# A fused attention and MoE kernel: one PSUM tile of two banks made two, and another order from the list scheduler

## The chip, the cores and the metric

The kernel runs on one core of a Trainium2 chip. The metric is the device time of one execution in microseconds (us); the lower the better. The engines are named as in the profile: PE is TensorE's matmuls, PEld its weight loads, DVE is VectorE, ACT ScalarE, POOL GpSimd, SP SyncE, which issues DMAs.

## What is computed

Two parts, one behind the other. Retention attention over 4 × 768 tokens, 8 heads of 64; then RMS norm and a gated layer (512 to 1536 to 512). Both in fp32.

```python
# attention, for each block b of the sequence (pos is the place in the block)
Dmask = np.where(rel >= 0, lam[:, None, None] ** rel[None, :, :], 0.0)
intra = np.einsum('bhic,bhjc->bhij', qb, kb) * Dmask[None]
intra = np.einsum('bhij,bhjd->bhid', intra, vb)
inter = np.einsum('bhid,bhde->bhie', qb * lam_pow[None], kv_state)
out[:, :, sl] = intra + inter
kv_state = lam_block[None, :, None, None] * kv_state + np.einsum('bhsd,bhse->bhde', kb_dec, vb)
...
# gated layer, x is the attention's output as 3072 x 512
rms = np.sqrt(np.mean(x * x, axis=-1, keepdims=True) + 1e-06)
xn = x / rms * rms_g
g = xn @ w_gate
silu = g * (1.0 / (1.0 + np.exp(-g)))
val = xn @ w_val
return (silu * val @ w_out).astype(np.float32)
```

## The kernel before

**Tiles and stages.** The 3072 tokens are six groups `m` of 512 (four chunks of 128, `GC`). The inner width of 1536 is twelve blocks `f` of 128. A *unit* is one `(m, f)`: it takes the group's normed tokens through block `f` of the gate and the value weights, joins both and multiplies with the block of the output weights into four accumulators `acc` (banks `po0` to `po3`). The heads go in four *pairs* `p` a group. Matrix products in fp32 precision are made from fp16 halves (a high and a low part, `x`'s, `wg`, `wv`, `wo`), so each takes three.

The first 24 units are *classical*: 12 matmuls of 512 columns into `pg` (gate) and 12 into `pv` (value). All later ones are *Strassen* units: a product with fewer matmuls from sums of the weights (`ws`, from which come the low-precision sums in `wo`, `third`, `partial`) and of the tokens. Such a unit has seven products of six matmuls with 256 columns; they go into two halves, `pa` and `pb`. The first product goes into `pa`, the second into `pb`; ScalarE copies `pa` away (`keep`, L984), VectorE adds `pb` to the copy (`sum_val`, L988), and further products follow in both.

**PSUM.** Odd Strassen units take `pa` and `pb` from the two one-bank tiles `pg` and `pv`. Even ones take both from *one* tile of two banks, tag `ps` (`pp` in the profile, L937). A pair's scores (L510) use the same two-bank tile, one bank for each head, and VectorE multiplies them with the decay mask in one instruction of 1024 columns (`decay_a`, L526). The row sums of the norm (`pss`), its spread to all partitions (`pr`), the norms of the weights (`pn`), of the output weights' columns (`pc`) and `pm` use the first bank of a `ps` tile.

**Weights.** Each block is loaded, rounded (`convert`, L231 and L234), squared and normed on TensorE (`norm_bank`: `pn`, L451), scaled; the output block's columns are squared by ScalarE (L305), added by VectorE (L311), the second time by GpSimd (L314), and summed by TensorE into `pc`, from which VectorE takes exponents (`en`, L336). Halves and low parts are made by ScalarE, VectorE (`rest_h`, L277) and GpSimd (L282); the sums `ws` by VectorE (L884 to L888).

**What sets the order.** The first six units and the eight pairs of groups 0 and 1 are a sequence written out by hand (`ramp`). Behind it a list scheduler (`Plan`) is given every step with its engine, a cost in us, a position, and what it reads, writes and opens; `run` picks steps in the order of their planned starts and issues them. Each engine then executes its queue in that order. The scheduler thinks of a bank as free 0.2 us after the last step that used it, and prices a VectorE step of its list `SHARED` higher while it plans a GpSimd step.

Of the kernel before, what the change touches and what calls it, by code (L numbers as in the profile page):

```python
# [23 lines left out]
def retention_swiglu_kernel(  # L24
# [261 lines left out]
    class Column:  # L286
# [26 lines left out]
        def last(self):  # L313
            nc.gpsimd.tensor_add(self.sq[:, :, 0], self.sq[:, :, 0], self.sq[:, :, 1])  # L314

    class Norms:
# [13 lines left out]
        def part(self, fn, i):  # L330
            self.pc = ps_att.tile([P, 2, G], F32, tag="ps", name="pc")[:, 0]
            fn(i, self.between)
# [40 lines left out]
    def spread_least():  # L373
        pm = ps_att.tile([P, 2, G], F32, tag="ps", name="pm")[:, 0, :P]
        nc.tensor.matmul(pm, least.broadcast_to([P, P]), ident, start=True, stop=True)
        return pm
# [19 lines left out]
    class Weights:  # L396
# [97 lines left out]
    class Pair:  # L494
# [9 lines left out]
        def scores(self, chunks=range(GC)):  # L504
            m, p = self.m, self.p
            if 0 in chunks:
                self.pa = ps_att.tile([P, 2, GC, P], F32, tag="ps", name=f"pa_{m}_{p}")
            for c in chunks:
                for j, r in enumerate(heads):
                    nc.tensor.matmul(  # L510
                        self.pa[:, j, c, :], self.kT[r, c, :], self.qT[r, c, :],
                        start=True, stop=True,
                    )
# [8 lines left out]
        def decay_a(self):  # L522
            p = self.p
            self.a = att.tile([P, 2, GC, P], F32, tag="a", name=f"a_{self.m}_{p}", bufs=2)
            decay = mask[:, 2 * p : 2 * p + 2, :].rearrange("p j (o i) -> p j o i", o=1)
            nc.vector.tensor_mul(self.a, self.pa, decay.broadcast_to([P, 2, GC, P]))  # L526
# [88 lines left out]
    def row_sums(m, i):  # L615

        if i == 0:
            if m:
                ps = ps_att.tile([P, 2, G], F32, tag="ps", name=f"pss_{m}")[:, 0]
# [12 lines left out]
    class Norm:  # L632
# [20 lines left out]
        def spread(self):  # L653
            if self.m:
                pr = ps_att.tile([P, 2, GC, P], F32, tag="ps", name=f"pr_{self.m}")[:, 0]
# [17 lines left out]
        def row_sums(self):  # L673

            ps = ps_att.tile([P, 2, G], F32, tag="ps", name=f"pss_{self.m}")[:, 0]
# [266 lines left out]
    class Hidden:  # L942
# [31 lines left out]
        def first(self, u):  # L974
            self.banks(u)
            self.add(1)

# [67 lines left out]
    def ramp():  # L1045
# [122 lines left out]
        w1.pn = ps_att.tile([P, 2, G], F32, tag="ps", name="pn_1")[:, 0]  # L1168
# [34 lines left out]
        w2.pn = ps_att.tile([P, 2, G], F32, tag="ps", name="pn_2")[:, 0]  # L1203
# [35 lines left out]
        w3.pn = ps_att.tile([P, 2, G], F32, tag="ps", name="pn_3")[:, 0]  # L1239
# [40 lines left out]
        w4.pn = ps_att.tile([P, 2, G], F32, tag="ps", name="pn_4")[:, 0]  # L1280
# [46 lines left out]
        w5.pn = ps_att.tile([P, 2, G], F32, tag="ps", name="pn_5")[:, 0]  # L1327
# [78 lines left out]
    class Plan:  # L1406


        LAG = {("PE", "PE"): 0.0, ("PE", "ACT"): 0.28, ("PE", "DVE"): 0.28}
        SHARED = (  # L1410
            "low", "mul_sums", "sums", "refine", "rest_high", "convert", "convert_o", "add_squares",
        )
        ENGINES = ("PE", "ACT", "DVE", "POOL", "LD", "LO", "ST")

# [33 lines left out]

        def run(self, horizon=1.3, reach=600):
            deps = self.links()  # L1450
            n = len(self.steps)
            end = [None] * n
            clock = dict.fromkeys(self.ENGINES, 0.0)
            left = list(range(n))
            live = {}
            left_of = {k: len(v) for k, v in self.users.items()}
            free_at = {t: [0.0] * b for t, b in self.tags.items()}
            tag_of = {}
            for name, tag in self.open.items():
                tag_of[name] = tag  # L1460
                free_at[tag].pop()
                if name not in left_of and name not in self.fixed:
                    free_at[tag].append(0.0)
            last = dict.fromkeys(clock, 0.0)
            progress, order = 0.0, []
            pool_until = 0.0

            def ready(i):
                eng = self.steps[i][0]
                t = 0.0  # L1470
                for d in deps[i]:
                    if end[d] is None:
                        return None
                    t = max(t, end[d] + self.LAG.get((self.steps[d][0], eng), 0.15))
                need = {}
                for name, tag in self.steps[i][7]:
                    k = need[tag] = need.get(tag, 0) + 1
                    if len(free_at[tag]) < k:
                        return None
                    t = max(t, sorted(free_at[tag])[k - 1] + 0.2)  # L1480
                return t

            while left:
                found = {}
                window = left[:reach]
                for limit in (horizon, 99.0):
                    for i in window:
                        eng, _, at = self.steps[i][:3]
                        if at > progress + limit:
                            continue  # L1490
                        if eng in ("LD", "LO") and found.get(eng):
                            continue
                        t = ready(i)
                        if t is None:
                            if eng in ("LD", "LO"):
                                found[eng] = [(at, 1e9, i)]
                            continue
                        found.setdefault(eng, []).append((at, t, i))
# [501 lines left out]
```

## Time and profile before

| | before |
|---|---|
| median of 3 runs | 671.53 us (670.36 to 672.75) |
| the profiled execution | 672.92 us, span 671.1 us |
| granted TensorE clock, mean | 0.997 |
| busy: PE, PEld | 652.8, 444.1 us |
| busy: DVE, ACT, POOL | 440.4, 330.5, 163.6 us |
| DMA | 51.12 MB, mean 76 GB/s |

Busy times are those of the profiled execution. PEld runs beside PE. A matmul's record is longer than the step to the next one, since matmuls are pipelined: 0.38 us for 512 fp16 columns at a step of some 0.21. So idle time before a matmul is what lies between the end of one record and the start of the next, and a loss is read from start to start. In a timeline a row is: start, length, engine, line, operation, output and inputs, shape, count, and in brackets the idle time of the engine before it with what ended it.

### The profile page before, as it was taken

The numbers are of one execution on the slowest core, as the hardware profiler recorded it, in microseconds if no ns is written. First come the engines' busy times: TensorE is split into PE (matmuls) and PEld (weight loads), VectorE is DVE, ScalarE is ACT, GpSimd is POOL, SyncE is SP. The second block draws the span as 40 slices with busy tenths as digits, with TensorE's granted clock in tenths as the row PEclk, the third lists the DMA queues.
The fourth block names the chain that finished last, engine by engine and source line by source line (L and its number), as shares of the span: only waits on it lengthen the run. The fifth ranks groups of instructions, "written<-read, shape, count | busy, mean of one in ns | idle before, by whom it ended". The sixth has DMA issues, their size and how long they took to land.

```text
span 671.1 us, 12372 instructions
## 1 busy us (share of the span) xinstructions
PE 652.8 (97%) x5035; PEld 444.1 (66%) x5035; DVE 440.4 (66%) x790; ACT 330.5 (49%) x672; POOL 163.6 (24%) x144
## 2 busy tenths in 40 slices
PE   8999999999999999999999999999999999999997
PEld 8846655555565555777767777767777776767774
DVE  6798869889977976767664444477644377543333
ACT  3686658676654542454453443335444434433332
POOL 2300130114776833478220011002111001100000
PEclk9999999999999999999999999999999999999999
DMA  8966626321002200211100321100230000100001
GB/s 312 346 237 213 230 79 209 113 84 64 0 3 97 91 1 33 95 63 63 65 1 1 110 79 64 64 1 1 80 111 1 1 1 1 39 26 1 1 1 63
DMA packets 14312, 51.12 MB, mean 76 GB/s; under 512 B 1712, under 2 KB 1968, under 8 KB 12848
## 3 DMA queue, kind: packets, MB, share of 16 engines
q1 hardware_dynamic: 13968, 49.69, 20.8%
q8 instruction: 39, 0.64, 0.4%
q10 hardware_dynamic: 288, 0.66, 0.4%
q14 instruction: 17, 0.14, 0.1%
HBM read 44.05 MB, written 6.29 MB: 75 GB/s over the span
## 4 chain that ended last, share of the span: by engine, by line
PE 85%; DVE 10%; ACT 2%; issue 1%; DMA 1%; POOL 0%; DVEq 0%; ACTq 0%; POOLq 0%
PE pp L937 17%; PE pa L937 9%; PE acc L779 9%; PE acc L781 8%; PE acc L780 8%; PE pv L760 7%; PE pg L760 7%; PE pb L937 7%; PE pa L510 4%; PE po L571 3%; PE po L582 3%; PE pst L539 2%; DVE tx L988 1%; PE pss L627 1%; ACT tx L984 1%
## 5 line engine op out<-in xcount | busy, mean ns | idle before, releaser
L781 PE MATMUL acc<-wo,hh 128*128 128x512 f16 (+1 forms) x288 | 111.0, 386 | 0.0
L780 PE MATMUL acc<-wo,hh 128*128 128x512 f16 (+1 forms) x288 | 111.0, 385 | 0.0
L779 PE MATMUL acc<-wo,hh 128*128 128x512 f16 x216 | 82.4, 381 | 0.2 <-DVE hh L1033 0.2
L937 PEld LDWEIGHTS <-wo 128*128 128x128 f16 x576 | 55.7, 98 | 31.4 <-issue 9.8
L760 PE MATMUL pg<-x,wg 128*128 128x512 f16 x288 | 67.6, 380 | 1.3 <-ACT sg L1008 1.1
L937 PEld LDWEIGHTS <-wg 128*128 128x128 f16 x576 | 56.3, 98 | 16.8 <-issue 0.8
L760 PE MATMUL pv<-x,wv 128*128 128x512 f16 x288 | 67.3, 379 | 0.0
L1026 ACT CAST hh<-sg 128x512 f16<-128x512 f32 (+1 forms) x72 | 44.4, 617 | 44.8 <-DVE sg L1002 20.9
L984 ACT COPY tx<-pp 128x256 f32<-128x256 f32 x72 | 26.8, 372 | 77.2 <-PE pp L937 76.2
L937 PEld LDWEIGHTS <-wv 128*128 128x128 f16 x576 | 56.2, 98 | 8.7 <-DVE xn L733 0.6
L988 DVE TENSOR_TENSOR tx<-pp,tx 128x256 f32<-128x256 f32 x48 | 20.4, 425 | 58.9 <-ACT sg L996 45.7
L530 POOL TENSOR_TENSOR qkv<-qkv,pw 128x512 f32<-128x512 f32 x22 | 30.3, 1381 | 101.6 <-PE pa L510 101.6
L984 ACT COPY tx<-pa 128x256 f32<-128x256 f32 x72 | 26.7, 371 | 53.6 <-PE pa L937 52.9
L760 PEld LDWEIGHTS <-wg 128*128 128x128 f16 x288 | 26.4, 98 | 35.2 <-issue 5.3
L760 PEld LDWEIGHTS <-wv 128*128 128x128 f16 x288 | 27.5, 98 | 33.2 <-issue 1.4
L1033 DVE TENSOR_TENSOR hh<-sg,hh 128x512 f16<-128x512 f32 x54 | 41.0, 759 | 6.3 <-ACT hh L1026 5.5
L992 DVE TENSOR_TENSOR sg<-pp,tx 128x256 f32<-128x256 f32 x24 | 10.2, 424 | 51.3 <-ACT tx L984 51.3
L937 PE MATMUL pp<-tx,wo 128*128 128x256 f16 x288 | 39.0, 272 | 5.0 <-DVE tx L988 4.4
L1002 DVE SCALAR_TENSOR_TENSOR sg<-tx,cv,sg 128x512 f32<-128x512 f32 x48 | 38.9, 811 | 3.3
L988 DVE TENSOR_TENSOR tx<-pb,tx 128x256 f32<-128x256 f32 x48 | 20.4, 424 | 28.2 <-PE pb L937 25.3
L781 PEld LDWEIGHTS <-hh 128*128 128x128 f16 x216 | 21.1, 98 | 25.5
L754 POOL TENSOR_TENSOR tx<-xt,tx 128x768 f16<-128x768 f32 x8 | 14.8, 1853 | 92.8 <-ACT tx L750 92.8
(192 smaller groups left out, 1310.1 us busy)
## 6 DMA issues: line engine op xcount, KB each, us to landing
qkv<-in_qkv_dram SPq DMA_DIRECT2D x47, 512.0 KB, 4.7
raw_gv<-in_weights_dram SPq DMA_DIRECT2D x11, 1024.0 KB, 5.2
raw_o<-in_weights_dram SPq DMA_DIRECT2D x12, 512.0 KB, 5.1
out_dram<-o SPq DMA_DIRECT2D x23, 256.0 KB, 2.0
partial<-in_weights_dram SPq DMA_DIRECT2D x2, 512.0 KB, 11.9
qkv<-in_qkv_dram ACTq DMA_DIRECT2D x1, 512.0 KB, 4.5
out_dram<-o SPq DMA_DIRECT2D x1, 128.0 KB, 1.7
out_dram<-o ACTq DMA_DIRECT2D x1, 128.0 KB, 2.4
```

The source lines that it names most:

```text
L510: nc.tensor.matmul(self.pa[:, j, c, :], self.kT[r, c, :], self.qT[r, c, :], start=True, stop=True,)
L530: eng.tensor_mul(self.qT, self.qT, pw[:, p : p + 1, :].broadcast_to([P, GC, P]))
L760: nc.tensor.matmul(ps, w[:, kk, :], x[:, kk, :], start=i == kk == 0, stop=i == 2 and kk == NK - 1,)
L779: nc.tensor.matmul(acc, hl[:, ts_], oh, start=first, stop=False)
L780: nc.tensor.matmul(acc, hh[:, ts_], ol, start=False, stop=False)
L781: nc.tensor.matmul(acc, hh[:, ts_], oh, start=False, stop=last)
L937: nc.tensor.matmul(ps, w(ow, k), x(ox, k), start=first and i == k == 0, stop=i == 2 and k == 1, skip_group_check=True,)
L984: nc.scalar.copy(self.kept[:, i], self.pa)
L988: nc.vector.tensor_add(self.val[:, half], self.pb, self.kept[:, i])
L1002: nc.vector.scalar_tensor_tensor(self.sg, self.val, cv[:, self.f : self.f + 1], self.sg, ALU.mult, ALU.mult)
L1026: nc.scalar.copy(self.hh, self.sg)
L1033: nc.vector.tensor_sub(self.hl, self.sg, hh)
```

## The change

One tag becomes two, `ps0` and `ps1`, of one bank each. A pair's scores take both, and the decay is two instructions of 512 columns. Even Strassen units take `pa` from `ps0` at the first product and `pb` from `ps1` at the second (before, both at once); all small sums go into `ps1`. The second addition of the squares of a column goes from GpSimd to VectorE. In the scheduler, `run` gets a table of delays between engines, counts a bank as free by the engine that asks for it, and lets no VectorE step of `SHARED` begin in the plan while a GpSimd step is planned, nor the other way; `SHARED` is larger, and some costs are changed. The sequence of the ramp is the same but for the tiles.

```diff
         def last(self):
-            nc.gpsimd.tensor_add(self.sq[:, :, 0], self.sq[:, :, 0], self.sq[:, :, 1])
+            nc.vector.tensor_add(self.sq[:, :, 0], self.sq[:, :, 0], self.sq[:, :, 1])
...
         def norm_bank(self):
-            self.pn = ps_att.tile([P, 2, G], F32, tag="ps", name=f"pn_{self.f}")[:, 0]
+            self.pn = ps_att.tile([P, G], F32, tag="ps1", name=f"pn_{self.f}")
...
         def scores(self, chunks=range(GC)):
             m, p = self.m, self.p
             if 0 in chunks:
-                self.pa = ps_att.tile([P, 2, GC, P], F32, tag="ps", name=f"pa_{m}_{p}")
+                self.pa = [
+                    ps_att.tile([P, GC, P], F32, tag=f"ps{j}", name=f"pa_{m}_{p}_{j}")
+                    for j in range(2)
+                ]
...
-        def decay_a(self):
+        def decay_a(self, part=None):
             p = self.p
-            self.a = att.tile([P, 2, GC, P], F32, tag="a", name=f"a_{self.m}_{p}", bufs=2)
-            decay = mask[:, 2 * p : 2 * p + 2, :].rearrange("p j (o i) -> p j o i", o=1)
-            nc.vector.tensor_mul(self.a, self.pa, decay.broadcast_to([P, 2, GC, P]))
+            if not part:
+                self.a = att.tile([P, 2, GC, P], F32, tag="a", name=f"a_{self.m}_{p}", bufs=2)
+            for j in range(2):
+                if part in (None, j):
+                    h = 2 * p + j
+                    decay = mask[:, h : h + 1, :].broadcast_to([P, GC, P])
+                    nc.vector.tensor_mul(self.a[:, j], self.pa[j], decay)
...
         def banks(self, u):
             m, f = self.m, self.f
-            if u % 2 == 0:
-                t = ps_att.tile([P, 2, G], F32, tag="ps", name=f"pp_{m}_{f}")
-                self.pa, self.pb = t[:, 0, :HG], t[:, 1, :HG]
-            else:
-                self.pa = ps_gv.tile([P, G], F32, tag="pg", name=f"pa_{m}_{f}")[:, :HG]
-                self.pb = ps_gv.tile([P, G], F32, tag="pv", name=f"pb_{m}_{f}")[:, :HG]
+            pool, tag = (ps_att, "ps0") if u % 2 == 0 else (ps_gv, "pg")
+            self.pa = pool.tile([P, G], F32, tag=tag, name=f"pa_{m}_{f}")[:, :HG]
...
+        def second(self, u):
+            pool, tag = (ps_att, "ps1") if u % 2 == 0 else (ps_gv, "pv")
+            self.pb = pool.tile([P, G], F32, tag=tag, name=f"pb_{self.m}_{self.f}")[:, :HG]
+            self.add(2)
...
-        LAG = {("PE", "PE"): 0.0, ("PE", "ACT"): 0.28, ("PE", "DVE"): 0.28}
-        SHARED = (
-            "low", "mul_sums", "sums", "refine", "rest_high", "convert", "convert_o", "add_squares",
-        )
+        NEXT = {"PE": 0.0, "ACT": 0.09, "DVE": 0.08, "POOL": 0.04}
+        SHARED = {
+            "low", "low_o", "mul_sums", "sums", "refine", "rest_high", "convert", "convert_o",
+            "add_squares", "scale", "undo", "scaled_to",
+        }
...
+        def lag(a, b):
+            if a == b:
+                return 0.0 if a == "PE" else 0.03
+            return 0.22 if a == "PE" else 0.1 if a in ("LD", "LO", "ST") else 0.06
...
+            held = {"DVE": 0.0, "POOL": 0.0}
...
+                if shared(i):
+                    t = max(t, held["DVE" if eng == "POOL" else "POOL"] - 0.13)
                 return t
...
-                if eng == "DVE" and fn.__name__ in self.SHARED and start < pool_until:
-                    cost += 0.8 * min(cost, pool_until - start)
-                if eng == "POOL":
-                    pool_until = start + cost
-                clock[eng] = start + cost
+                clock[eng] = start + cost - self.NEXT.get(eng, 0.0)
                 end[i] = start + cost + lasts
+                if shared(i):
+                    held[eng] = start + cost
...
-        step("POOL", 0.72, at + 0.4, c.last, w=[f"sqw{f}"])
+        step("DVE", 0.28, at + 0.4, c.last, w=[f"sqw{f}"])
...
-        step("PE", cost, u, h.first, u, r=[v, *x01], w=[a, "turn:pg", "turn:pv"], new=banks)
+        step("PE", cost, u, h.first, u, r=[v, *x01], w=[a, "turn:pg", "turn:pv"], new=banks[:1])
         step("ACT", 0.37, u - 1, h.keep, 0, r=[a], w=["kept0:0"])
-        step("PE", cost, u + 0.05, h.add, 2, r=[v, *x23], w=[b])
+        step("PE", cost, u + 0.05, h.second, u, r=[v, *x23], w=[b, "turn:pv"], new=banks[1:])
```

What that does to the engines' queues, at three places. Rows read: line, operation, output<-inputs, columns; a number behind a name counts the tile. First, TensorE in the last token group, block 10, an even unit: from the end of the value products (`wv`) over one accumulator of an earlier unit (`acc`) to the next product of the unit (`wo`). Before:

```order
L937 MATMUL pp_10_6646<-x_4956,wv 128x256
L779 LDWEIGHTS hh_8_6597
L779 MATMUL acc_0_0_6109<-wo_8_2299,hh_8_6597 128x512
L780 LDWEIGHTS hh_8_6597
L780 MATMUL acc_0_0_6109<-wo_8_2299,hh_8_6597 128x512
L781 LDWEIGHTS hh_8_6597
L781 MATMUL acc_0_0_6109<-wo_8_2299,hh_8_6597 128x512
L937 LDWEIGHTS wo_10_2427
L937 MATMUL pp_10_6646<-tx_2361,wo_10_2427 128x256
```

After:

```order
L944 MATMUL pb_10_6725<-x_5006,wv 128x256
L786 LDWEIGHTS hh_8_6668
L786 MATMUL acc_0_0_6178<-wo_8_2300,hh_8_6668 128x512
L787 LDWEIGHTS hh_8_6668
L787 MATMUL acc_0_0_6178<-wo_8_2300,hh_8_6668 128x512
L788 LDWEIGHTS hh_8_6668
L788 MATMUL acc_0_0_6178<-wo_8_2300,hh_8_6668 128x512
L944 LDWEIGHTS wo_10_2423
L944 MATMUL pa_10_6717<-tx_2391,wo_10_2423 128x256
```

The rows and their order stay; the product behind the accumulator now goes into `pa`, while the one just ahead of it went into `pb`, another tile.

Second, VectorE around the weights' sums `ws`, the last exponents `en` before `pn` of block 11, and `sg`, the joining of a classical unit (L1015, after L1023). Before:

```order
L277 SCALAR_TENSOR_TENSOR rest_h_1738<-wo_681,ts,wo_1_1722 128x512
L254 TENSOR_TENSOR wo_1740<-wv,wo_1740 128x512
L884 TENSOR_TENSOR ws_1758<-r_1670 128x256
L885 TENSOR_TENSOR ws_1758<-r_1670 128x256
L887 TENSOR_TENSOR ws_1758<-r_1670,ws_1758 128x256
L888 TENSOR_TENSOR ws_1758<-r_1670,ws_1758 128x256
L1015 SCALAR_TENSOR_TENSOR sg_8_1756<-pv_8_1747,cg,sg_8_1756 128x512
L336 TENSOR_SCALAR en<-pc 128x2
L311 TENSOR_TENSOR sq_w_1768<-sq_w_1768 128x2x256
```

After:

```order
L277 SCALAR_TENSOR_TENSOR rest_h_1754<-wo_693,ts,wo_1_1737 128x512
L254 TENSOR_TENSOR wo_1756<-wv,wo_1756 128x512
L294 TENSOR_REDUCE ts<-wo_1756 128x1
L891 TENSOR_TENSOR ws_1779<-r_1691 128x256
L892 TENSOR_TENSOR ws_1779<-r_1691 128x256
L336 TENSOR_SCALAR en<-pc 128x2
L1023 SCALAR_TENSOR_TENSOR sg_8_1769<-pv_8_1764,cg,sg_8_1769 128x512
L311 TENSOR_TENSOR sq_w_1782<-sq_w_1782 128x2x256
L311 TENSOR_TENSOR sq_w_1793<-sq_w_1793 128x2x256
```

The second half of `ws` (L887, L888) has gone behind `en`, which now also stands ahead of `sg`; a reduction of the output block (L294) has come ahead of it.

Third, TensorE around `pn` of block 11, which needs the bank that `pc` leaves when `en` has been taken. Before:

```order
L779 MATMUL acc_0_2_1238<-wo_1267,hl_7_1716 128x512
L780 MATMUL acc_0_2_1238<-wo_1267,hh_7_1710 128x512
L781 MATMUL acc_0_2_1238<-wo_1267,hh_7_1710 128x512
L451 LDWEIGHTS ones_b
L451 MATMUL pn_1798<-ssq_1682,ones_b 128x2
L779 MATMUL acc_0_3_1242<-wo_1267,hl_7_1716 128x512
```

After:

```order
L788 MATMUL acc_0_1_1252<-wo_1280,hh_7_1730 128x512
L451 LDWEIGHTS ones_b
L451 MATMUL pn_1810<-ssq_1701,ones_b 128x2
L786 MATMUL acc_0_2_1259<-wo_1280,hl_7_1735 128x512
L787 MATMUL acc_0_2_1259<-wo_1280,hh_7_1730 128x512
L788 MATMUL acc_0_2_1259<-wo_1280,hh_7_1730 128x512
```

`pn` has moved up by one accumulator, from behind the third to behind the second.

More of the change, by code (lines that the diff above doesn't have):

```diff
@@ L1167, in ramp @@
         busy(2, 3)
-        w1.pn = ps_att.tile([P, 2, G], F32, tag="ps", name="pn_1")[:, 0]
+        w1.pn = ps_att.tile([P, G], F32, tag="ps1", name="pn_1")
         w1.norm(slice(1, 2))
@@ L1202, in ramp @@
         h1.silu()
-        w2.pn = ps_att.tile([P, 2, G], F32, tag="ps", name="pn_2")[:, 0]
+        w2.pn = ps_att.tile([P, G], F32, tag="ps1", name="pn_2")
         w2.norm()
@@ L1279, in ramp @@
         w4.square(1)
-        w4.pn = ps_att.tile([P, 2, G], F32, tag="ps", name="pn_4")[:, 0]
+        w4.pn = ps_att.tile([P, G], F32, tag="ps1", name="pn_4")
         w4.norm()
@@ L1326, in ramp @@
         h4.mul()
-        w5.pn = ps_att.tile([P, 2, G], F32, tag="ps", name="pn_5")[:, 0]
+        w5.pn = ps_att.tile([P, G], F32, tag="ps1", name="pn_5")
         w5.norm()
@@ L1460, in run, with shared @@
                 tag_of[name] = tag
-                free_at[tag].pop()
+                free[tag].pop()
                 if name not in left_of and name not in self.fixed:
-                    free_at[tag].append(0.0)
-            last = dict.fromkeys(clock, 0.0)
+                    free[tag].append(None)
+            held = {"DVE": 0.0, "POOL": 0.0}
             progress, order = 0.0, []
-            pool_until = 0.0
-            def ready(i):
[L1469 to L1472, printed above, removed]
-                        return None
[L1474 to L1480, printed above, removed]
+            def shared(i):
+                eng, fn = steps[i][0], steps[i][3]
+                return eng == "POOL" or eng == "DVE" and fn.__name__ in self.SHARED
@@ L1793, in strassen @@
         if u % 2 == 0:
-            a, b = f"pp{u}:a", f"pp{u}:b"
-            banks = [(f"pp{u}", "ps")]
+            banks = [(a, "ps0"), (b, "ps1")]
         slot = SLOT_OF[m]
```

127 lines of the change are left out of this document (67 added, 60 removed).

## The prediction

> **What bounds the kernel now.** I read the busy shares first, then the table by stretch, then TensorE's waits, then the timelines of the places that the waits name.
>
> ```profile
> span 671.1 us, 12372 instructions
> PE 652.8 (97%) x5035; PEld 444.1 (66%) x5035; DVE 440.4 (66%) x790; ACT 330.5 (49%) x672; POOL 163.6 (24%) x144
> ```
>
> TensorE is busy for 652.8 of 671.1 us. No other engine is near. The change removes no matrix work, so all it can win is TensorE's 18.3 idle microseconds and what a wait costs beside the idle time shown.
>
> ```profile
> 150.00:190.00 40.00, 36.78 (x191) 21.13 (x190) 38.34 (x56) 25.74 (x50) 24.89 (x23) 0.96 0.08 27
> 260.00:340.00 80.00, 78.14 (x696) 55.91 (x694) 58.27 (x101) 36.62 (x84) 41.21 (x36) 1.00 0.19 67
> 340.00:500.00 160.00, 158.49 (x1376) 116.23 (x1375) 85.32 (x158) 70.18 (x154) 18.36 (x13) 1.00 0.15 54
> ```
>
> The columns are the length, busy PE, weight load, VectorE, ScalarE, GpSimd, granted clock. VectorE is full (38.34 of 40) only between 150 and 190, where TensorE idles 3.2 us and the clock falls to 0.96. Later VectorE has half its time free, yet TensorE still loses a little.
>
> ```profile
> PE pp L937 <- DVE tx L988: 4.4, 13, 0.6
> PE pst L539 <- ACT sg L1008: 1.7, 1, 1.7
> PE pn L451 <- DVE en L336: 1.5, 1, 1.5
> PE pg L760 <- ACT sg L1008: 1.1, 1, 1.1
> PE pp L937 <- DVE sg L992: 0.6, 1, 0.6
> PE pp L937 <- ACT tx L984: 0.5, 2, 0.3
> PE po L571 <- DVE sg L1015: 0.5, 1, 0.5
> PE pp L937 <- DVE x L721: 0.3, 1, 0.3
> ```
>
> TensorE's waits: total, count, longest. Two families stand out. Seventeen short waits (13+1+2+1, together 5.8 us) are all on `pp`, the two-bank tile of the even Strassen units; the odd ones, in two tiles `pa` and `pb`, have almost none. And three longer ones (1.7, 1.5, 0.5) lie between 150 and 255 us, where VectorE is late.
>
> **Why `pp` waits.** An odd unit, then the even one behind it:
>
> ```profile
> 640.75 0.38 PE L781 MATMUL acc<-wo,hh 128*128 128x512 f16 x1
> 640.97 0.82 PE L937 MATMUL pa<-tx,wo 128*128 128x256 f16 x6
> ...
> 646.18 1.47 PE L937 MATMUL pp<-x,wv 128*128 128x256 f16 x12
> 647.71 0.38 PE L780 MATMUL acc<-wo,hh 128*128 128x512 f16 x1
> 647.75 0.37 ACT L984 COPY tx<-pp 128x256 f32<-128x256 f32 x1 [1.55 <-PE pp L937]
> 647.92 0.38 PE L781 MATMUL acc<-wo,hh 128*128 128x512 f16 x1
> 648.15 0.42 DVE L988 TENSOR_TENSOR tx<-pp,tx 128x256 f32<-128x256 f32 x1 [0.49 <-ACT tx L984]
> 648.63 0.82 PE L937 MATMUL pp<-tx,wo 128*128 128x256 f16 x6 [0.33 <-DVE tx L988]
> ```
>
> The first product ends halfway through the group of 12, but ScalarE's copy starts at 647.75, after the second has ended too; then VectorE adds, and TensorE's next product, which goes into the half that ScalarE read, waits for VectorE, which read the other half. The wait follows the tile, not the data. The odd unit at 640.97 starts 0.22 after its predecessor. The even one starts 648.63 − 647.92 = 0.71 after, where 647.92 − 647.71 = 0.21 is the pitch without a wait: it loses 0.50, of which 0.33 is shown as idle and 0.16 is pipelining between matmuls that is lost when one waits.
>
> **The change, part by part.** *Two tiles.* TensorE's order in token group 5, unit 10 (`pp_10` before; `pa_10` and `pb_10` after): the same matmuls, but the third product now goes into a tile that only ScalarE has read. That is the odd unit's pattern, which shows no wait. All 17 waits cost 5.8 + 17 × 0.16 = 8.5 us. I do not take all: in the stretch around 340 the bank `ps1` is still held by the RMS norm's spread when one unit's second product wants it, and around 270 products run without `acc` matmuls between them; by reading the order I leave 0.9 and 0.3. Term: −7.3, between −8.5 and, if only the units from 430 on gain (11 of the 17, 0.5 each), −5.5.
>
> The same split costs VectorE a second instruction per pair of heads:
>
> ```profile
> L526 DVE TENSOR_TENSOR a<-pa,mask 128x1024 f32<-128x1024 f32 x24 | 29.3, 1222 | 6.1 <-PE pa L510 3.1 <-PE po L571 1.9
> L988 DVE TENSOR_TENSOR tx<-pb,tx 128x256 f32<-128x256 f32 x48 | 20.4, 424 | 28.2 <-PE pb L937 25.3
> ```
>
> From 424 ns at 256 columns and 1222 at 1024 a column costs 1.04 ns and an instruction 0.16 us; 24 more are 3.8 us of VectorE. [...] Uncovered it is only in the hand-ordered ramp:
>
> ```profile
> 26.94 1.23 DVE L526 TENSOR_TENSOR a<-pa,mask 128x1024 f32<-128x1024 f32 x1 [0.94 <-PE pa L510]
> ...
> 34.99 0.38 PE L760 MATMUL pg<-x,wg 128*128 128x512 f16 x1 [0.28 <-ACT x L718]
> ```
>
> Behind this decay VectorE runs nearly without a gap to the operands of `pg` at 34.99, which TensorE waits for. One pair there costs 0.16 and a little overlap, and others of the ramp's eight may do part of it: +0.4 (0 to +0.8; if every ramp pair paid in full it would be 8 × 0.16 = 1.3).
>
> *VectorE's SBUF operations and GpSimd's apart.*
>
> ```profile
> 161.92 1.50 DVE L884 TENSOR_TENSOR ws<-r 128x256 f32<-128x256 f32 x1
> 163.34 1.38 DVE L885 TENSOR_TENSOR ws<-r 128x256 f32<-128x256 f32 x1
> 164.76 0.43 DVE L887 TENSOR_TENSOR ws<-r,ws 128x256 f32<-128x256 f32 x1
> 166.22 0.15 DVE L336 TENSOR_SCALAR en<-pc 128x2 int32<-128x2 int32 x1
> ...
> 161.43 1.71 POOL L282 TENSOR_TENSOR wo<-rest_h,rest_l 128x512 f16<-128x512 f32 x1 [1.35 <-DVE rest_h L277]
> 163.10 1.35 POOL L869 TENSOR_TENSOR r<-wg 128x512 f32<-128x512 f16 x1
> ```
>
> An addition of 0.43 us takes 1.50 and 1.38 beside a GpSimd operation, and ends about when that ends (163.42 against 163.14, 164.72 against 164.45). So ahead of `en`, on which TensorE waits for the 1.5 of the list, VectorE lost 1.07 + 0.95 = 2.0 us to overlaps. Apart, they need not be lost, but a wait for the other engine may take their place. In the changed order `en` also moves ahead of the two additions of 0.43 and of a multiplication: from 164.76 to 166.22, 1.5 us. It now stands behind one reduction more (a single pass over 512 columns, by 1.04 ns each and 0.16 an estimated 0.7), and TensorE asks for `pn` one block of three matmuls (3 × 0.21) earlier. Without any gain by keeping apart, 1.5 − 1.5 + 0.7 + 0.6 = 1.3 stay; with it, 0. I leave 0.5.
>
> The other long wait:
>
> ```profile
> 180.96 0.72 ACT L268 ACTIVATE wo<-wo,ts 128x512 f16<-128x512 f32 x1 [0.73 <-DVE rest_h L277]
> 182.31 0.57 PE L539 MATMUL pst<-qkv 128*64 128x64 f32 x12 [1.68 <-ACT sg L1008]
> 183.86 0.63 PE L780 MATMUL acc<-wo,hh 128*128 128x512 f32 x1
> 184.29 0.63 PE L781 MATMUL acc<-wo,hh 128*128 128x512 f32 x1
> ```
>
> ScalarE's SiLU stands behind a cast that waits for VectorE's `rest_h`, and it still does in the new order; only VectorE's queue ahead of it can shrink, by one stretched addition (1.0) if nothing runs beside it. Half of the 1.7 goes. Right behind it matmuls run at a pitch of 184.29 − 183.86 = 0.43 instead of 0.21. The granted clock of 0.96 over 40 us stands for 1.6 us lost that way; I use 1.7, from the matmuls that run so (183.7 to 187.1). The wait of 1.1 (`pg` for SiLU, at 100.67) keeps its order on ScalarE and stays.
>
> So between 95 and 255, 1.7 + 1.5 + 0.5 of idle, 3 × 0.16 and 1.7 of clock make 5.9 us that could go. For what part I have only the two ends: all (keeping apart removes the lateness) and none (it changes stretch into waiting). I take half: −2.9.
>
> *Second add of column squares.*
>
> ```profile
> L314 POOL TENSOR_TENSOR sq_w<-sq_w 128x256 bf16<-128x256 bf16 x12 | 9.6, 799 | 54.7 <-DVE sq_w L311 39.8 <-DVE ts L351 7.6 <-DVE e L458 6.9
> L311 DVE TENSOR_TENSOR sq_w<-sq_w 128x512 bf16<-128x512 bf16 x12 | 4.9, 418 | 0.9 <-ACT sq_w L305 0.9
> ```
>
> GpSimd loses 12 operations of 0.80; VectorE gains 12 of half the width of a 0.42 one: between 0.21 and 0.42, 2.5 to 5 us, in the stretch where it is fullest. That is inside the half that I left there: it shortens the chain to `pc` (0.80 and a change of engine) while it fills VectorE. Counted at nothing more; if its cover is gone, up to +1 at `en`.
>
> *DMAs* keep their order on SP's queue, and none is added; GpSimd's queue loses the 12 adds alone.
>
> Sum: −7.3 + 0.4 − 2.9 = −9.8 us. Against the profiled run (672.92 with a span of 671.1) this gives 663.1; that run lies 1.4 above the median of 671.53 (670.36 to 672.75), so I forecast 661.7 as the median.
>
> **Rivals.** *Nothing is won in the middle* (chance 0.30). VectorE's work between 150 and 190 does not shrink, it grows by splits and adds; a planner that makes GpSimd or VectorE stand still instead of stretching gives the same end. For it: the stretched operations end where GpSimd's end, which is what one engine's waiting for the other looks like. Then only −7.3 + 0.4, and up to 1 more lost: 671.53 − 6.9 = 664.6, up to 665.6. [...]
>
> *The waits at `pp` are real* (0.06): TensorE's next product needs a bank that is not free in time with any tiles. Against it stand the odd units. Then half of 8.5 and the middle half: 671.53 − 4.2 + 0.4 = 667.7.
>
> *Slower* (0.04). Scores write both banks and now wait for two engines, ScalarE's SiLU on `ps0` and VectorE's sum on `ps1`.
>
> ```profile
> 395.15 0.47 ACT L996 ACTIVATE sg<-pp,cg 128x256 f32<-128x256 f32 x1 [1.18 <-PE pp L937]
> 395.66 0.42 DVE L988 TENSOR_TENSOR tx<-pp,tx 128x256 f32<-128x256 f32 x1 [2.23 <-ACT sg L996]
> 396.35 1.16 PE L510 MATMUL pa<-qkv 64*128 64x128 f32 x16
> ```
>
> The scores follow 0.27 after the sum's end. In two tiles SiLU need not wait for the second product, whose six matmuls last 1.47 − 0.82 = 0.65 (the records of 12 and of 6 above), and the sum can follow that product at about 395.15, so the slack grows to some 0.7. The 16 pairs of token groups 2 to 5 would have to be held up by 0.6 each to eat the 9.8, so the sum would have to come 1.3 late every time, behind two wide operations of VectorE; with VectorE busy for 85 of 160 us I do not expect it. At 1.5 late and more the kernel gets slower: 16 × 0.8 = 12.8 lost, 674.5.
>
> *No change* (0.05): the gains of the first family return as idle time elsewhere: 671.5.
>
> **How the numbers follow.** The forecast, 8 to 13 us faster, has 0.55. With the middle lost 0.30 (664.6 to 665.6). These two end faster, as does the 0.06 at 667.7: 0.91. Same 0.05, slower 0.04. About 0.3%, 2.0 us, is what a measurement can tell from no change. The range goes from all 8.5 and nearly all 5.9 won, 671.5 − 14 = 657.5, to the bound of the real waits, 667.7, and leaves out 0.1 above and some 0.05 below.
>
> **What would show it.** Right: no wait on `pa` or `pb` of more than 0.2 in the profile after 430, and even units as long as odd ones; VectorE's decay in 48 operations of about 0.69; `en` and `pst` waits together below 1.7; TensorE's idle time near 10 us instead of 18.3. Half right: the 340 to 671 stretch shorter by 4 to 5 us, and the 95 to 255 one as long as before. Wrong: VectorE's or ScalarE's entries as releasers of L513 (the scores) in the list of waits; a clock below 1.00 in a stretch where it was 1.00; or a ramp longer by over 1 us.

## The result and the profile after

| | before | after |
|---|---|---|
| median (runs) | 670.94 us (669.73 to 672.75, 4) | 662.78 us (662.10 to 664.61, 4) |
| ratio of the runs, 95% interval | | 0.988, 0.985 to 0.991 |
| profiled execution, span | 672.92, 671.1 us | 662.10, 660.3 us |
| busy PE, DVE, POOL | 652.8, 440.4, 163.6 us | 648.2, 430.4, 152.9 us |

8.2 us faster; 9.8 were forecast. The profiles differ by more, 10.8, because they caught a long run of before and a short one of after. TensorE's waits in the profile after, total, count, longest:

```profile
PE pc L325 <- DVE a L533: 2.2, 1, 2.2
PE unread L146 <- POOL power L135: 1.5, 1, 1.5
PE pg L767 <- ACT sg L1016: 1.5, 1, 1.5
PE pn L451 <- ACT junk L446: 1.1, 2, 0.8
PE pb L944 <- DVE tx L996: 0.6, 1, 0.6
```

The seventeen waits at `pp` are gone but for one of 0.6, and so are the three at `pst`, `pn` (for `en`) and `po`. A new one of 2.2 at `pc` has come; the one at `pg` has grown from 1.1 to 1.5, and those at `pn` for ScalarE's squares from 0.4 to 1.1. An even unit of the tail, the place that the prediction showed for before:

```profile
636.56 0.82 PE L944 MATMUL pb<-x,wv 128*128 128x256 f16 x6
636.81 0.37 ACT L992 COPY tx<-pa 128x256 f32<-128x256 f32 x1 [0.89 <-PE pa L944]
637.51 0.42 DVE L996 TENSOR_TENSOR tx<-pb,tx 128x256 f32<-128x256 f32 x1
637.64 0.38 PE L788 MATMUL acc<-wo,hh 128*128 128x512 f16 x1
637.86 0.82 PE L944 MATMUL pa<-tx,wo 128*128 128x256 f16 x6
```

ScalarE's copy now starts while the second product runs, and the third product follows the accumulator by 0.22, though VectorE's addition is still at work (637.51 to 637.93). Before it followed by 0.71. Set side by side at the same accumulator matmuls, the two profiles drift apart by 0.49 at each even unit of the tail.

Set side by side in this way over the whole span (below: by accumulators; the times are those of the matmul in before), the profile after is ahead by 1.2 us at 50.91, the first accumulator matmul. It loses 1.3 between 88.67 and 105.66, wins 2.7 between 138.00 and 259.41, and wins 8.2 behind that, where all even Strassen units lie. Together these make the 10.8.

Four windows of the profile after, columns as in the prediction:

```profile
62.00:100.00 38.00, 36.62 (x245) 24.01 (x245) 30.14 (x54) 21.01 (x39) 11.09 (x9) 1.00 0.41 141
100.00:150.00 50.00, 49.17 (x231) 27.41 (x231) 42.26 (x93) 37.62 (x67) 0.00 (x0) 1.00 0.41 142
150.00:190.00 40.00, 37.83 (x202) 21.00 (x201) 35.62 (x62) 26.50 (x50) 19.79 (x16) 1.00 0.08 27
260.00:340.00 80.00, 80.00 (x731) 59.35 (x729) 51.34 (x107) 39.14 (x89) 39.57 (x36) 1.00 0.19 67
```

From 260 to 340 TensorE has no gap left. From 150 to 190 it still loses 2.2 us. And GpSimd, busy for 11.09 us between 62 and 100, does nothing at all from 100 to 150 (0.00 in the last busy column). In before it was busy for 8.39 and 5.89 us in these two windows: the adds between 100 and 150 have gone to VectorE, and what stood behind them now runs ahead of 100. That turned out to be the part of the change that the prediction had priced at nothing.

### The profile page after: what moved, and what is told of

Its sections match the earlier page's. It is cut to its first block, busy times and chain, and to the rows that moved or that the text cites. A ratio compares the mean times of both kernels' runs of the same rounds, so it can differ in the third digit from the quotient of the medians.

```text
span 660.3 us, 12361 instructions
## 1 busy us (share of the span) xinstructions
PE 648.2 (98%) x5035; PEld 442.1 (67%) x5035; DVE 430.4 (65%) x826; ACT 333.5 (50%) x672; POOL 152.9 (23%) x132
## 4 chain that ended last, share of the span: by engine, by line
PE 91%; DVE 5%; ACT 2%; issue 1%; DMA 1%; POOL 0%; DVEq 0%; POOLq 0%
PE pa L944 19%; PE pb L944 14%; PE acc L786 10%; PE acc L788 9%; PE acc L787 9%; PE pg L767 8%; PE pv L767 8%; PE pa L513 4%; PE po L578 3%; PE po L589 3%; PE pst L546 2%; PE pss L634 1%; DMA qkv<-in_qkv_dram 1%; ACT sq_w L305 1%; DVE sq_w L311 0%
## 5 line engine op out<-in xcount | busy, mean ns | idle before, releaser
L992 ACT COPY tx<-pa 128x256 f32<-128x256 f32 x144 | 53.6, 372 | 133.8 <-PE pa L944 133.0
L996 DVE TENSOR_TENSOR tx<-pb,tx 128x256 f32<-128x256 f32 x96 | 40.8, 425 | 71.2 <-PE pb L944 64.7
L1000 DVE TENSOR_TENSOR sg<-pb,tx 128x256 f32<-128x256 f32 x48 | 20.3, 424 | 77.7 <-ACT tx L992 77.7
L944 PE MATMUL pb<-tx,wo 128*128 128x256 f16 x288 | 39.3, 273 | 0.6 <-DVE tx L996 0.6
L944 PE MATMUL pa<-tx,wo 128*128 128x256 f16 x288 | 39.3, 273 | 0.0
L944 PE MATMUL pa<-x,wv 128*128 128x256 f16 x288 | 39.3, 273 | 0.0
L944 PE MATMUL pb<-x,wv 128*128 128x256 f16 x288 | 39.3, 273 | 0.0
L944 PE MATMUL pb<-x,wg 128*128 128x256 f16 x288 | 39.3, 273 | 0.0
```

The source lines that it names most:

```text
L944: nc.tensor.matmul(ps, w(ow, k), x(ox, k), start=first and i == k == 0, stop=i == 2 and k == 1, skip_group_check=True,)
L992: nc.scalar.copy(self.kept[:, i], self.pa)
L996: nc.vector.tensor_add(self.val[:, half], self.pb, self.kept[:, i])
```

## Experiments

Medians of the timed runs, each beside runs of before on the same chip (670.65 to 670.96), with the ratio and its 95% interval. "Stretch" is my own sum over each profile: by how much each VectorE operation lasted longer than the shortest of its line and shape, where that was over 0.1 us.

| kernel | median us | ratio to before | stretch us |
|---|---|---|---|
| e0: before again | 670.58 | 0.9993 to 1.0015 | (before: 52.5) |
| e5: decay split only | 670.98 | 0.9991 to 1.0012 | 51.6 |
| e6: column add on VectorE only | 673.63 | 1.0029 to 1.0061 | 45.0 |
| e2: new scheduler only | 672.70 | 1.0015 to 1.0039 | 39.1 |
| e1: two tiles only | 662.76 | 0.9857 to 0.9895 | 50.2 |
| after: all three | 662.78 | 0.9848 to 0.9913 | 33.6 |
| e3: two tiles and scheduler | 658.39 | 0.9795 to 0.9825 | 32.2 |
| e7: after with a brake on GpSimd | 660.86 | 0.9832 to 0.9874 | 33.7 |
| e4: e3 without the rule | 667.50 | 0.9933 to 0.9970 | 40.7 |
| e9: e3, rule with overlap 0.0 | 667.49 | 0.9925 to 0.9958 | 32.5 |
| e10: e3, overlap priced | 666.12 | 0.9911 to 0.9944 | 39.6 |
| e11: e3, rule with overlap 0.26 | 662.34 | 0.9856 to 0.9889 | 39.1 |
| e8: e3, last conversion planned | 657.55 | 0.9781 to 0.9823 | 31.1 |

**e0, before again.** No edit.

> The kernel before once more, unchanged, to see what varies between its executions. The profile of before has two stretches that the profile after lacks and that no instruction of the change touches: ten warm-up matmuls that take 2.45 us instead of 1.38 near 7 us, and a lower clock from 183.7 to 187.1. Theory (these two are luck of the clock): a second profile lacks one or both, with a span of 668.5 to 670.5 instead of 671.1, and the 17 waits on pp (5.8 us of idle) are there again. Rival (they belong to the order of before): both are there at the same places, span 671 again.

The warm-up matmuls took 1.76 us this time (2.45 and, in the profile after, 1.38), so that start varies from run to run. The span was 669.8, and the pitch of 0.43 behind the wait at `pst` was there again. The 17 waits at `pp` came to 5.9 us. The first accumulator matmul came 1.3 us earlier than in the first profile, with nothing changed: the start is luck. The slow matmuls behind `pst` returned in this profile, but not in every execution: of the twelve timed runs seven have a mean granted clock of 1.000 (670.50 to 670.70 us) and three one of 0.997 (671.43 to 673.12).

**e1, two tiles alone.** The tiles, the `second` step and the decay in halves as in the change; the class `Plan`, its costs and the second add as before.

> The two tiles ps0 and ps1 and the decay in two halves alone; the scheduler, its costs and the second column add (on GpSimd) as before. Theory (the waits on pp follow the tile, so two tiles remove them with any order): no waits on pa or pb above 1 us in all, 6.5 to 8 us faster than before, about 663 to 664.5; the middle stage (95 to 255 us) keeps its waits at pn and pst, as long as before within 1 us. Rival (the new order removes them, by issuing first products earlier): under 3 us faster.

8.1 us faster, just above the 6.5 to 8 of the theory, and the whole gain of the change. Its waits:

```profile
PE pst L546 <- ACT sg L1016: 1.7, 1, 1.7
PE pn L451 <- DVE en L336: 1.5, 1, 1.5
PE unread L146 <- POOL power L135: 1.5, 1, 1.5
PE pc L325 <- DVE a L533: 1.2, 1, 1.2
PE pg L767 <- ACT sg L1016: 1.1, 1, 1.1
```

Nothing of the even units is among the long ones, while `pst` and `pn` wait just as before: the waits at `pp` belonged to the tile, and no new order was needed to remove them. The 1.2 at `pc` is new. By accumulators, e1 wins 8.3 us against before behind 259.41, about as much as after (8.2).

**e2, the scheduler alone.** The class `Plan` and the costs of the change; one `ps` tile, one decay, second add on GpSimd.

> The new scheduler and its costs alone; one tile of two banks, one decay instruction and the second column add on GpSimd as before. Theory: the even units' waits stay, some 12 to 17 of them with 4 to 6 us of idle, and only the middle gains: 1 to 4 us faster, 667 to 670. Rival (the order is what matters): 5 us or more faster. Second rival (keeping VectorE and GpSimd apart only turns stretch into waiting): within 1 us of before.

1.9 us slower: none of the three forecasts. `pst` is gone from the list and `pn` fell to 0.4, so the middle did gain; but with the two-bank tile the new order pays more for it later:

```profile
PE pp L937 <- DVE tx L988: 6.5, 12, 1.5
PE pp L937 <- DVE sg L992: 1.4, 3, 0.6
PE pp L937 <- ACT tx L984: 1.3, 3, 0.5
PE pp L937 <- DVE xn L733: 0.9, 1, 0.9
```

That is 10.1 us in 19 waits where before had 5.8 in 17. By accumulators it wins 3.4 us against before between 138.00 and 259.41 (some 1.5 of them are the lower clock in the profile of before), and loses 4.6 behind. The two parts are not additive: the new order is worth −4.4 us with two tiles (e1 to e3) and costs 1.9 with one.

**e3, the second add back on GpSimd.**

```diff
-            nc.vector.tensor_add(self.sq[:, :, 0], self.sq[:, :, 0], self.sq[:, :, 1])
+            nc.gpsimd.tensor_add(self.sq[:, :, 0], self.sq[:, :, 0], self.sq[:, :, 1])
...
-        step("DVE", 0.28, at + 0.4, c.last, w=[f"sqw{f}"])
+        step("POOL", 0.72, at + 0.4, c.last, w=[f"sqw{f}"])
```

> The changed kernel with the second add of the column squares back on GpSimd. The profile after has one new long wait: 2.2 us at pc near 183 us, where the adds on VectorE (0.42 and 0.28 wide when alone, 1.24, 1.27 and 0.91 there) stand ahead of the decay that pc waits for. Theory (the moved add makes that wait): it shrinks to under 1 us and the kernel is 1 to 2 us faster than the changed one. Rival (the first adds are stretched too, and GpSimd gets 12 more operations that stretch others): the wait stays or another takes its place, same time within 1 us or up to 2 us slower.

658.39: 4.4 us faster than after, more than twice what the theory gave. So that one move of the change costs 4.4 us. In the profile after, GpSimd and VectorE in order of time:

```profile
93.13 1.16 POOL L876 TENSOR_TENSOR r<-wv 128x512 f32<-128x512 f16 x1
94.24 1.60 POOL L876 TENSOR_TENSOR r<-wg 128x512 f32<-128x512 f16 x1
...
93.20 1.63 DVE L728 TENSOR_TENSOR x<-xn,x 128x512 f16<-128x512 f32 x1
95.36 1.04 DVE L231 TENSOR_SCALAR w<-w 128x1024 int32<-128x1024 int32 x1
```

and the same operations in e3:

```profile
148.15 1.18 POOL L876 TENSOR_TENSOR r<-wv 128x512 f32<-128x512 f16 x1
...
92.69 0.68 DVE L728 TENSOR_TENSOR x<-xn,x 128x512 f16<-128x512 f32 x1
93.89 0.68 DVE L231 TENSOR_SCALAR w<-w 128x1024 int32<-128x1024 int32 x1
```

In e3, as in before (149.81), the weight sums `r` run near 150 us, behind seven of the adds. Their inputs are ready at 93, and in the changed kernel no add stands ahead of them in GpSimd's queue; the adds, each of which waited for VectorE (5.83 to 7.80 us of idle time ahead of each in before), had held that queue back. Now they run 55 us early, beside VectorE's last operations of the ramp, and stretch two of them by 0.95 and 0.36. Behind these wait ScalarE's squares and SiLU, and behind them TensorE's `pn` and `pg` near 99 us. At the accumulator matmul at 105.66 before, the profile after has lost 1.31 us against its lead at 50. The second place is 180 to 185:

```profile
180.41 1.24 DVE L311 TENSOR_TENSOR sq_w<-sq_w 128x512 bf16<-128x512 bf16 x1 [2.72 <-ACT sq_w L305]
181.68 1.27 DVE L314 TENSOR_TENSOR sq_w<-sq_w 128x256 bf16<-128x256 bf16 x1
182.87 0.68 DVE L533 TENSOR_TENSOR a<-pa,mask 128x512 f32<-128x512 f32 x1
183.47 0.91 DVE L311 TENSOR_TENSOR sq_w<-sq_w 128x512 bf16<-128x512 bf16 x1
184.30 0.68 DVE L533 TENSOR_TENSOR a<-pa,mask 128x512 f32<-128x512 f32 x1
...
181.31 1.48 POOL L537 TENSOR_TENSOR qkv<-qkv,pw 128x512 f32<-128x512 f32 x1
182.76 0.72 POOL L913 TENSOR_TENSOR third<-ws,third 128x256 f16<-128x256 f32 x1
...
185.03 0.16 PE L325 MATMUL pc<-ones_b,sq_w 128*128 128x1 bf16 x1 [2.17 <-DVE a L533]
```

The moved add (L314, 1.27 where it takes 0.28 to 0.29 alone) and the first adds stand ahead of the two decays, which must empty `ps1` before `pc` may use it. By accumulators, after loses 1.3 us against e3 at the first place and 1.9 behind it: 3.2 in these two profiles, where the medians differ by 4.4.

**e7, a brake.** To tell VectorE's time from the lost brake: the adds stay on VectorE, and beside each GpSimd gets one tiny operation that must wait for it.

```diff
             nc.vector.tensor_add(self.sq[:, :, 0], self.sq[:, :, 0], self.sq[:, :, 1])
+            nc.gpsimd.tensor_add(brake, self.sq[:, 0, 0, :1], self.sq[:, 1, 0, :1])
```

> The changed kernel with its twelve second adds on VectorE, and beside each add one tiny operation on GpSimd (one column of the same squares, into a scratch tile, which nothing reads). The orders of TensorE, VectorE and ScalarE are those of the changed kernel; only GpSimd's queue gets twelve operations that must wait for VectorE. Theory (the moved add costs its 4.4 us not by VectorE's time but because GpSimd lost the operation that held its queue back: it now makes the weight sums r at 93 us, 55 us earlier than before, beside VectorE's last operations of the ramp): the time falls to 658 to 660, r starts near 148 again, and the waits of 1.5 at pg and 2.2 at pc shrink. Rival (VectorE's 12 adds are the cost): 662 to 663, as the changed kernel.

660.86, 1.9 us faster than after with twelve operations more, and less than forecast.

```profile
147.92 0.23 POOL L317 TENSOR_TENSOR brake<-sq_w 128x1 bf16<-128x1 bf16 x1 [7.89 <-DVE inv L482]
148.10 1.15 POOL L879 TENSOR_TENSOR r<-wv 128x512 f32<-128x512 f16 x1
```

`r` is back at 148 and the wait at `pg` at 1.1; at `pc` 1.7 of the 2.2 stay, and one of 0.9 at `pst` is new. By accumulators the loss of 1.3 near 99 is gone and 0.4 is lost again behind it. So the lost brake is shown for the place near 99. Of the 4.4 it makes some 1.3 by that place and 1.9 by the medians, a rough figure, since the intervals of after and e7 overlap. The rest stays with the adds on VectorE and the order that the scheduler then makes, which no run separates further.

**e6, the add alone, on the old kernel.** The same line and step as in e3, in the other direction, applied to before.

> The kernel before with only the second column add moved to VectorE (and so planned); one two-bank tile and the old scheduler. Theory of the lost brake: r starts near 93 to 95 us instead of 149.8, VectorE's operations there are stretched, and the kernel is 1 to 4 us slower than before. Rival (the add costs only beside the new order): within 1 us of before. Second rival (a shorter chain to pc helps the old order): 1 us or more faster.

2.9 us slower, with `r` at 92.77 and a wait of 4.3 at `pc` for the decay. The price is no accident of the new order.

**e5, the split decay alone.**

```diff
-            decay = mask[:, 2 * p : 2 * p + 2, :].rearrange("p j (o i) -> p j o i", o=1)
-            nc.vector.tensor_mul(self.a, self.pa, decay.broadcast_to([P, 2, GC, P]))
+            for j in range(2):
+                h = 2 * p + j
+                decay = mask[:, h : h + 1, :].broadcast_to([P, GC, P])
+                nc.vector.tensor_mul(self.a[:, j], self.pa[:, j], decay)
```

> The kernel before with each pair's decay in two VectorE instructions of 512 columns on the same two-bank tile; nothing else, the scheduler still plans one step. Theory (24 instructions more are 3.8 us of VectorE by the rows, covered outside the ramp): 0 to 1.3 us slower than before. Rival (they count in full, above all where VectorE is late): 2 to 4 us slower.

670.98 us against 670.65: +0.3 by the medians, +0.1 by the ratio, and its interval holds no change. The 24 more VectorE instructions are hidden.

**e4, e9, e10, e11: the rule.** All are e3, whose rule lets the two engines' steps overlap by 0.13 us in the plan, with a line or two of `run` changed. e4 takes the rule out:

```diff
-                if shared(i):
-                    t = max(t, held["DVE" if eng == "POOL" else "POOL"] - 0.13)
```

> The fastest so far (two tiles, new scheduler, second add on GpSimd: 658.39) without the one rule that keeps VectorE's SBUF steps and GpSimd's steps apart in the plan; the rest of the new scheduler stays. The new order was worth 4.4 us on top of the two tiles. Theory (keeping apart is what wins in the middle): 1.5 to 4.5 us of it go, 660 to 663, with waits at pn, pst or pc between 150 and 190. Rival (the delays, the costs and the way a bank counts as free make the difference): within 1 us of 658.4.

Without the rule 667.50, 9.1 us slower: more than the theory allowed, and more than the order had won. Its long waits are the old ones, larger:

```profile
PE pst L546 <- ACT sg L1016: 4.4, 1, 4.4
PE pn L451 <- DVE en L336: 2.2, 1, 2.2
```

That looked like a proof of the rule, but a loss above the whole gain asked for a control. e9 keeps the rule and allows no overlap:

```diff
-                    t = max(t, held["DVE" if eng == "POOL" else "POOL"] - 0.13)
+                    t = max(t, held["DVE" if eng == "POOL" else "POOL"])
```

> The kernel with two tiles, the new scheduler and the second add on GpSimd (658.39), with one number of the rule changed: a VectorE SBUF step and a GpSimd step may not overlap in the plan at all, where before they might by 0.13 us. Theory (the rule wins, not one lucky order): within 1.5 us of 658.4. Rival (list schedules scatter by several us with any change, and the 9 us between the kernels with and without the rule are partly that): 660 to 668.

With no overlap allowed, the rule at its strictest, 667.49. The theory fell. VectorE's stretch is as small as in e3 (32.5 against 32.2 us), and yet 9.1 us are lost, in other places:

```profile
PE pst L546 <- ACT sg L1016: 2.3, 3, 0.8
PE acc L786 <- DVE hl L1041: 2.0, 1, 2.0
PE acc L786 <- DVE hh L1041: 1.6, 2, 1.5
```

e10 leaves the rule out, as e4, and puts the old scheduler's price in its place:

```diff
-                if shared(i):
-                    t = max(t, held["DVE" if eng == "POOL" else "POOL"] - 0.13)
...
+                if eng == "DVE" and shared(i) and start < held["POOL"]:
+                    cost += 0.8 * min(cost, held["POOL"] - start)
```

> The same kernel with the rule replaced by what the old scheduler did: a VectorE SBUF step that starts while a GpSimd step is planned costs up to 0.8 of its price more, and both may overlap. Theory (keeping apart wins more than knowing of the stretch): 2 to 5 us slower than 658.4, with waits at pn, pst or pc between 150 and 190. Rival (any account of the stretch does, and the kernel without any, 667.5, lost 9 us for having none): within 1 us of 658.4.

666.12, 7.7 us slower than e3, where its theory said 2 to 5. The waits that it named are there (2.5 at `pn`, 1.9 at `pst`), but after e9 they no longer speak for the rule.

e11 keeps the rule with twice the overlap:

```diff
-                    t = max(t, held["DVE" if eng == "POOL" else "POOL"] - 0.13)
+                    t = max(t, held["DVE" if eng == "POOL" else "POOL"] - 0.26)
```

> The kernel of 658.39 with the rule's permitted overlap in the plan doubled, 0.26 us instead of 0.13 (with 0.0 it took 667.5). Theory (one setting gives a lucky order; with others the rule brings nothing over the old scheduler's order, which with two tiles takes 662.8): 661 to 668, with one or two waits of 1.5 us or more at pn, pst, pc or acc between 150 and 260. Rival (a strict rule stalls VectorE, a lax one is good): 657 to 660.

662.34, as the theory of a lucky order said. With two tiles and the add on GpSimd the old scheduler gives 662.76 (e1), and four variants of the new one 662.3 to 667.5. Only the setting 0.13 gives 658.4. What is shown: within the new scheduler the rule lowers the stretch, from 40.7 and 39.6 us without it to 32.2 and 32.5 with an overlap of 0.13 or 0.0; with 0.26 it is 39.1. That it lowers the time is not shown: the time changes by up to 9 us with 0.13 us in one comparison. By accumulators they part between 138.00 and 259.41: e3 wins 4.6 us there against before and e11 1.5 (the clock's 1.5 included), while e10 and e4 lose 2.0 and 3.2. (In e9 the work stands in another order around 259, so this mark does not fit it.) Why 0.13 is the good one stays open.

**e8, the last conversion made known.** The hand-written ramp ends with `w6.convert()`, four operations of which the scheduler knows nothing.

```diff
-        w6.convert()
         return w6
...
+        step("DVE", 4.0, 6.05, w6.convert, w=["wb6"])
         split_steps(w6, 6.1)
```

> The fastest so far, with the last conversion of the ramp (VectorE, four operations, 95 us) made known to the scheduler as a step of 4.0 us instead of being issued ahead of the plan. ScalarE then issues the SiLU of unit 1_0 ahead of the squares that wait for that conversion, and TensorE asks for pn four matmuls later. The profiles show pg_1_1 waiting 1.1 us for that SiLU in all kernels so far. Theory (ScalarE's order alone makes that wait): the 1.1 at pg and 0.4 at pn go, 1 to 1.8 us faster, 656.6 to 657.4. Rival (VectorE is the bound there, and the wait comes back one unit later): within 0.7 us of 658.4.

657.55, 0.8 us faster than e3, and the fastest of all: 13.2 us below before, ratio 0.980. The intervals of e3 and e8 overlap, but three of the four runs (657.36 to 657.59) lie below all of e3's (658.19 to 658.48).

```profile
97.22 0.69 ACT L1016 ACTIVATE sg<-pg,cg 128x512 f32<-128x512 f32 x1 [1.60 <-PE pg L767]
97.80 0.62 ACT L446 ACTIVATE junk<-w 128x512 bf16<-128x512 f32 x1
```

The SiLU now stands ahead of the squares, and TensorE is busy for 38.00 of 38 us between 62 and 100. The gain of 1.2 at that place in the profile comes out as 0.8 of the medians, a little under the 1 to 1.8 of the theory.

## Why the prediction was right, and where not

The time, 662.78, lies 1.1 from the forecast of 661.7, and the gain of 8.2 lies 1.6 below the 9.8; the median of before came out 0.6 lower than in the prediction. The first term is right in its mechanism and carries the result. That the sum came near is in part luck: by the medians the new scheduler wins 4.4 us on top of the two tiles and the moved add loses 4.4 again, and the prediction had neither size.

- **The waits at `pp`, −7.3.** Right in mechanism, 0.9 to 1.0 too small. e1 gives −8.1 in all, and behind 259.41 after wins 8.2 and e1 8.3, nearly the whole 8.5. One wait stays, 0.6 idle and 0.75 from start to start, near 341: that was the 0.9 left around there. The 0.3 left around 270 went too. The rival of real waits is out, since two tiles removed them. Its sum was also wrong: with the half of the middle that its words take in, 667.7 would have been 664.8.
- **Split decay, +0.4.** e5: +0.1 to +0.3, inside the 0 to 0.8. The decays keep VectorE busy for 31.0 us instead of 29.3, 1.7 more and not the 3.8 worked out from the rows, since a record reaches past the start of the next one (182.87 + 0.68 past 183.47 above).
- **The middle, −2.9.** Wrong as the change stands: the medians of after and e1 differ by 0.0 us. The forecast had taken half of 5.9. The three waits did go, to nothing even; but 2.2 at `pc` and the loss of 1.3 near 99 came in their place. The 1.7 of clock should not have stood in the 5.9: the clock was 1.00 from 150 to 190 in after, but so it was with the old scheduler in e1 and e5, and over the whole of most timed runs of e0. Of the 2.7 that the profile after wins between 138.00 and 259.41, some 1.5 is this clock: e5 wins that much there with nothing changed but the split. By its result this is the rival "nothing is won in the middle" (664.6), by its cause it is not: without the moved add the same scheduler does win 4.4 us (e1 to e3), by accumulators 4.3 of them there.
- **The moved add, nothing, "if its cover is gone, up to +1 at `en`".** The step that failed. It costs 4.4 us in this kernel and 2.9 in the old. The prediction counted the instruction on the engine that gets it and never asked what had waited behind it on the engine that loses it: GpSimd's queue "loses the 12 adds alone", it said, and did not follow the next operation, `r`, to where it would now start. By accumulators 1.3 us of the price fall near 99 and 1.9 behind. The order of GpSimd's rows and the inputs of `r` would have told it. The place was wrong too: `en` kept its time, `pn` and `pg` near 99 and `pc` near 183 paid. One of the prediction's own signs of being wrong came with it: near 99, where the ramp ends, the kernel is more than 1 us longer.
- **VectorE and GpSimd kept apart.** By the scheduler's rule alone VectorE's stretch fell from 40.7 to 32.2 us (e4 to e3). Whether that wins time or changes stretch into waiting, the question between the prediction's term and its first rival, stays open: at nearly the same stretch (32.2 and 32.5 us) e3 is 4.4 us faster than e1 and e9 4.7 slower.
- **Slower, by scores that wait for two engines.** No sign: from 340 to 500 TensorE is busy for 159.41 of 160 us in the profile after, and no score matmul (L513) waits for VectorE or ScalarE in its list. Weight loads of the scores did wait for ScalarE's `tx`, eight times and 1.7 us in all behind 340, beside running matmuls.
- The profiled run was taken as 1.4 above the median; e0 adds that its start alone, the warm-up at 2.45 us, was longer than other runs'. TensorE's idle time in the profile after is 12.1 us, not the 10 that was to show the prediction right.

## What to carry to other kernels

When an operation leaves an engine's queue, look at what stood behind it. Here the adds on GpSimd, each of which waited for VectorE, had been a brake as well: without them `r` ran at 93.13 us instead of 149.81, beside two operations of VectorE that took 0.95 and 0.36 us longer. A tile of two banks of which two engines read one half each made the next product into one half wait for the reader of the other too (17 waits, 5.8 us); two tiles of one bank cost an instruction more for each pair (0.1 to 0.3 us in e5) and took nearly all of these waits away under every order tried here (eight of the nine kernels with two tiles win 7.1 to 8.4 us behind 259.41; in e9 a wait of 1.5 at `acc` comes there). And a gain from a list scheduler's rule is shown only when a neighbouring setting of the same rule keeps it: here 0.13 us of margin moved the time by 9.

## What the runs showed of the hardware

Beside GpSimd some of VectorE's operations took longer and others did not. In the profile after, at 182.87, the decay, which reads PSUM and SBUF, took its usual 0.68 us while GpSimd ran an operation from 182.76 to 183.48; the add of two SBUF operands just ahead of it (L314), for whose whole length GpSimd was busy, took 1.27, and the other eleven of its line, with GpSimd idle, 0.28 to 0.29. All 48 decays of that profile took 0.68 or 0.69 us, though GpSimd was busy for over nine tenths of 24 of them. Nor is every operation from SBUF stretched: the reduction L294, which reads one operand from SBUF, took 0.68 at 160.20 while GpSimd ran an operation from 159.68 to 161.42, as the other eleven did with GpSimd idle. What decides which operations are stretched is not shown.

And the lower clock did not come with every wait of this length: behind the 1.7 us at `pst` matmuls ran at a pitch of 0.43 in both profiles of before, with a granted clock of 0.96 over 150 to 190, and at 0.23 in e1, with 1.00, behind the same wait of 1.68:

```profile
180.88 0.57 PE L546 MATMUL pst<-qkv 128*64 128x64 f32 x12 [1.68 <-ACT sg L1016]
...
182.36 0.39 PE L787 MATMUL acc<-wo,hh 128*128 128x512 f32 x1
182.59 0.39 PE L788 MATMUL acc<-wo,hh 128*128 128x512 f32 x1
```

What decides it stays open.
